# Twelve units of the second feed-forward network: the denominator's linear term and product on VectorE, and another order of the last three token tiles

## The chip, the cores and the metric

The kernel runs on one core of a Trainium2 chip. The metric is the device time of one execution in microseconds (us). The three runs of the kernel before took 796.35, 797.74 and 798.19 us; their median is 797.74. Times in the text are counted from the start of the span, the time from the first to the last instruction of the profiled execution.

## The reference

Attention, a mixture of experts and a second feed-forward network follow one another on 1152 tokens of 512 values, all in float32. The change touches the second network alone:

```
h = x @ w_in                                # 1152 x 512 @ 512 x 2048
P = a[0] + a[1]*h + a[2]*h**2 + a[3]*h**3
Q = 1 + |b[0]|*|h| + |b[1]|*h**2
g = P / (Q + 1e-6)
out = g @ w_out                             # 1152 x 2048 @ 2048 x 512
```

## The kernel before

Each factor of a matrix product is split into a high and a low part in a reduced format, and a product is made of three matmuls (high x high, high x low or low x high, and the third). TensorE accumulates in PSUM.

The 2048 hidden values of the second network are worked in four blocks of 512 (`blk` from `NB1`), the tokens in three groups of 384 (`q`), and a block's hidden values in four slices of 128 (`f`). One slice of one group is called a unit here; a block has twelve, numbered 0 to 11 for the first block. For each unit `first` issues twelve matmuls of 384 columns (line 1172) into a PSUM tile `ps_h`, of which there are three, and starts `rational`, which is a generator of three steps. At each new unit `step_stages` takes the third step of the unit two before it, the second of the one before, and the first of the new one, so each engine's queue holds these in that order. Step one: ScalarE makes `ha` = |h| (L1148), `pp` = a3*h + a2 (L1149) and `qq` = c1*|h| + c0 (L1150), the denominator's linear term; VectorE makes the numerator's next factors (L1151, L1152), which read `ps_h`; GpSimd multiplies `qq` by `ha` (L1153). Step two: ScalarE takes Ln and Exp (L1157, L1158) into `rr`, a tile in PSUM, and VectorE refines the reciprocal and makes the quotient (L1159, L1160, L1161). Step three: ScalarE copies the high part (L1163), GpSimd subtracts to get the low part (L1164).

`second` multiplies a group's four slices by `w_out` for one token tile of 128 tokens: twelve matmuls of 512 columns (L1180), the third, sixth, ninth and twelfth with low parts. In the first block ScalarE copies the result to `acc` (L1191); in later blocks VectorE adds it (L1193). In the last block each token tile is sent to the output from SP's queue. Token tiles 4 and 8 need two transfers each (L1199), the others one (L1201).

The first block overlaps the end of the mixture of experts: `down` for the last pair (VectorE's accumulation is L936), and `x2_T`, nine times, once for a token tile: four transpositions (L1207) into a PSUM tile of the same tag `r` and the same two slots as `rr`, a copy on ScalarE (L1209) and a subtraction on VectorE (L1210). The ninth comes after unit 4. From unit 5 on, each of six units also takes one weight chunk (`load_w`): a conversion to the high part on ScalarE (L298) and two subtractions on GpSimd for the low part (L304). The remaining chunks come in the later blocks, or with the units just before them.

The order of instructions is written out by hand; each engine works its queue in order, and waits are put in for data and for free buffers. At the end the three token tiles of the last group (6, 7, 8) are worked together: three slices of each tile, then the fourth slice of tile 6 and its output, of tile 7, of tile 8.

Of the kernel before, what the change touches and what calls it, by code (L numbers as in the profile page):

```python
# [9 lines left out]
F32 = mybir.dt.float32  # L10
# [3 lines left out]
AF = mybir.ActivationFunctionType  # L14
ALU = mybir.AluOpType
# [4 lines left out]
NT, DM = B * S, H * D  # L20
E, FF, FF2 = 4, 1024, 2048
NB = (E * FF + FF2) // 512
NB1 = E * FF // 512
NPAIR = E * FF // 256
P = 128
# [110 lines left out]
class Kernel:  # L136
# [992 lines left out]
    def second_stage(self):  # L1129
        nc, moe, acc = self.nc, self.wmoe, self.acc  # L1130
        self.o_bufs = 3
        x2 = self.xall.rearrange("p (w q k s) -> p w q k s", w=2, q=3, k=4)
        x2 = {q: (x2[:, 0, q], x2[:, 1, q]) for q in range(3)}
        a0, a1, a2, a3 = (self.ab[:, i:i + 1] for i in range(4))
        c0, c1 = self.babs[:, 0:1], self.babs[:, 1:2]

        stages = []

        def step_stages():
            for g in list(stages):  # L1140
                if next(g, True):
                    stages.remove(g)

        def rational(ps, hi, lo):
            def tmp(nm):
                return moe.tile([P, 384], F32, tag=nm, bufs=3, name=nm)
            ha, pp, qq = tmp("ha"), tmp("pp"), tmp("qq")
            nc.scalar.activation(out=ha, in_=ps, func=AF.Abs)  # L1148
            nc.scalar.activation(out=pp, in_=ps, func=AF.Identity, scale=a3, bias=a2)  # L1149
            nc.scalar.activation(out=qq, in_=ha, func=AF.Identity, scale=c1, bias=c0)  # L1150
            nc.vector.tensor_tensor(out=pp, in0=ps, in1=pp, op=ALU.mult)  # L1151
            nc.vector.scalar_tensor_tensor(out=pp, in0=pp, scalar=a1, in1=ps, op0=ALU.add, op1=ALU.mult)  # L1152
            nc.gpsimd.tensor_tensor(out=qq, in0=qq, in1=ha, op=ALU.mult)  # L1153
            yield False

            rr = self.ps.tile([P, 512], F32, tag="r", bufs=2, name="rr")[:, 0:384]
            nc.scalar.activation(out=rr, in_=qq, func=AF.Ln, bias=self.one_eps)  # L1157
            nc.scalar.activation(out=rr, in_=rr, func=AF.Exp, scale=-1.0)  # L1158
            nc.vector.scalar_tensor_tensor(out=qq, in0=qq, scalar=1.0 + 1e-6, in1=rr, op0=ALU.add, op1=ALU.mult)  # L1159
            nc.vector.scalar_tensor_tensor(out=rr, in0=qq, scalar=2.0, in1=rr, op0=ALU.subtract, op1=ALU.mult, reverse0=True)  # L1160
            nc.vector.scalar_tensor_tensor(out=pp, in0=pp, scalar=a0, in1=rr, op0=ALU.add, op1=ALU.mult)  # L1161
            yield False
            nc.scalar.activation(out=hi, in_=pp, func=AF.Copy)  # L1163
            nc.gpsimd.tensor_tensor(out=lo, in0=pp, in1=hi.bitcast(F32), op=ALU.subtract)  # L1164

        def first(blk, q, f):
            ps = self.ps.tile([P, 384], F32, tag="h", bufs=3, name="ps_h")
            (wh, wl), (hi_x, lo_x) = self.w_tiles["u", blk, f // 2], x2[q]
            fo = P * (f % 2)
            for k in range(4):  # L1170
                for i, (w, v) in enumerate(((wh, hi_x), (wh, lo_x), (wl, hi_x))):
                    nc.tensor.matmul(ps, lhsT=w[:, k, fo:fo + P], rhs=v[:, k, :], start=(k == i == 0), stop=(k == 3 and i == 2))  # L1172
            stages.append(rational(ps, *self.h_tiles(blk, q, f)))
            step_stages()

        def second_part(ps, blk, q, tt, f):
            hh, hl = self.hs[blk, q, f]
            wh, wl = self.w_tiles["d", blk, f // 2]
            for i, (a, w) in enumerate(((hh, wh), (hh, wl), (hl, wh))):
                nc.tensor.matmul(ps, lhsT=a[:, P * tt:P * tt + P], rhs=w[:, f % 2, :], start=(f == i == 0), stop=(f == 3 and i == 2))  # L1180

        def second(blk, q, tt):
            ps = self.ps.tile([P, DM], F32, tag="o", bufs=3, name="ps_o")
            for f in range(4):
                second_part(ps, blk, q, tt, f)
            second_out(ps, blk, q, tt)

        def second_out(ps, blk, q, tt):
            tok = 3 * q + tt
            if blk == NB1:  # L1190
                nc.scalar.activation(out=acc[:, tok], in_=ps, func=AF.Copy)  # L1191
            else:
                nc.vector.tensor_tensor(out=acc[:, tok], in0=ps, in1=acc[:, tok], op=ALU.add)  # L1193
                if blk == NB - 1:
                    out = self.t["out"]
                    if tok in (4, 8):
                        for to, rows in self.token_rows(out):
                            if to[1] == tok:
                                nc.sync.dma_start(out=rows, in_=acc[to])  # L1199
                    else:  # L1200
                        nc.sync.dma_start(out=out[P * tok:P * tok + P, :], in_=acc[:, tok])  # L1201

        def x2_T(q, tt):
            xh, xl = x2[q]
            ps = self.ps.tile([P, 4, P], F32, tag="r", bufs=2, name="ps_x")
            for k in range(4):
                nc.tensor.transpose(ps[:, k, :], acc[:, 3 * q + tt, P * k:P * k + P], self.ident)  # L1207
            sl = slice(P * tt, P * tt + P)
            nc.scalar.activation(out=xh[:, :, sl], in_=ps, func=AF.Copy)  # L1209
            nc.vector.tensor_tensor(out=xl[:, :, sl], in0=ps, in1=xh[:, :, sl].bitcast(F32), op=ALU.subtract)  # L1210

        units = [(blk, q) for blk in range(NB1, NB) for q in range(3)]
        F = [u + (f,) for u in units for f in range(4)]
        total = len(F)
        loads = []

        def up():
            blk, q, f = F.pop(0)
            first(blk, q, f)
            if loads:  # L1220
                loads.pop(0)()
            if (q, f) == (2, 3):
                loads.extend([self.load_w] * 2)

        def lead(n):
            while F and total - len(F) < n:
                up()


        p = NPAIR - 1  # L1230
        self.down(p - 1, 7)
        self.down(p - 1, 8)
        self.load_w()
        self.load_w()
        for t in range(9):
            self.down(p, t)
            if t:
                x2_T((t - 1) // 3, (t - 1) % 3)
            if t in (2, 4):
                self.load_w()  # L1240
            if t > 4:
                up()
        up()
        x2_T(2, 2)
        loads = [self.load_w] * 6
        for i, (blk, q) in enumerate(units[:-1]):
            for tt in range(3):
                lead(4 * i + tt + 7)
                if not F:
                    step_stages()  # L1250
                    step_stages()
                second(blk, q, tt)
            lead(4 * i + 9)
            if q == 2:
                loads.extend([self.load_w] * 2)

        blk, q = units[-1]
        ps = [self.ps.tile([P, DM], F32, tag="o", bufs=3, name="ps_o") for _ in range(3)]
        while stages:
            step_stages()  # L1260
        for tt in range(3):
            for f in range(3):
                second_part(ps[tt], blk, q, tt, f)
        for tt in range(3):
            second_part(ps[tt], blk, q, tt, 3)
            second_out(ps[tt], blk, q, tt)


@with_exitstack
# [46 lines left out]
```

## Time and profile before

| what | value |
|---|---|
| median of three runs | 797.74 us (796.35 to 798.19) |
| span of the profiled execution | 795.7 us |
| TensorE busy in the span | 774.5 us (97%) |
| VectorE, ScalarE, GpSimd busy | 647.8, 477.1, 467.5 us |
| mean granted clock of TensorE | 0.997 |
| last addition on VectorE ends | 791.96 us |

The profiled execution's own time is known as its span, 795.7 us, 2.04 us under the median of the runs. Busy shares are means over stages with different limits; the second network stands from about 583 us to the end. Matmuls overlap, so that a matmul's modelled end lies after the start of the next.

### The profile page before, as it was taken

What the parts mean: (1) busy time and instruction counts of PE and PEld (TensorE: products, weight loads), DVE (VectorE), ACT (ScalarE), POOL (GpSimd) and SP (SyncE); (2) the same over time, 40 slices, a digit from 0 to 9 for tenths busy, and PEclk for the clock granted to TensorE, in tenths of its full rate; (3) what the DMA queues carried; (4) which work ended last, traced back from release to release, by engine and by line L of the source; (5) the groups of instructions that cost most, each with busy time, mean ns of one, the idle gap of its engine ahead of it and who ended that gap; (6) DMA issues with size and microseconds to landing.
All of it is one profiled execution on the core that took longest, in us unless ns stands there. A gap on an engine that the chain in (4) does not pass through costs nothing.

```text
span 795.7 us, 13247 instructions
## 1 busy us (share of the span) xinstructions
PE 774.5 (97%) x4756; PEld 680.7 (86%) x4756; DVE 647.8 (81%) x1207; ACT 477.1 (60%) x940; POOL 467.5 (59%) x456
## 2 busy tenths in 40 slices
PE   6998999999999999999999999999999999999997
PEld 2338899998998999899988999889888889999986
DVE  7996899989779888888888888888577667888775
ACT  3878999999433333343333333333279998887772
POOL 4197798987366445555444564444257977754442
PEclk9999999999999999999999999999999999999999
DMA  6797758571014344443434443433131311000012
GB/s 163 266 309 184 205 125 212 116 217 38 22 33 132 120 132 133 133 133 106 130 110 133 133 133 114 137 99 101 41 107 42 118 53 54 2 1 1 0 41 79
DMA packets 70449, 87.63 MB, mean 110 GB/s; under 512 B 34288, under 2 KB 42736, under 8 KB 70256
## 3 DMA queue, kind: packets, MB, share of 16 engines
q1 hardware_dynamic: 69808, 86.63, 36.2%
q8 instruction: 37, 0.61, 0.3%
q14 instruction: 28, 0.23, 0.1%
q10 hardware_dynamic: 576, 0.16, 0.1%
HBM read 60.15 MB, written 21.61 MB: 103 GB/s over the span
## 4 chain that ended last, share of the span: by engine, by line
PE 76%; POOL 6%; ACT 6%; issue 5%; DVE 4%; DMA 2%; SPq 1%; ACTq 0%; POOLq 0%; DVEq 0%
PE ps_o L930 20%; PE ps_y L1022 10%; PE ps_o L1180 10%; PE ps_h L1172 9%; PE ps_x L1022 8%; PE ps L627 5%; PE ps L731 4%; PE ps L687 4%; POOL we L304 2%; PE ps_ab L436 1%; POOL wml L304 1%; PE ps_x L920 1%; DVE hid L426 1%; DMA bias_d<-bo 1%; PE ps L581 1%
## 5 line engine op out<-in xcount | busy, mean ns | idle before, releaser
L930 PE MATMUL ps_o<-we,hs 128*128 128x512 f32 x810 | 203.4, 392 | 0.0
L930 PEld LDWEIGHTS ps_o<-we,hs 128*128 128x128 f32 x810 | 146.0, 188 | 25.8
L304 POOL TENSOR_TENSOR we<-wstg,we 128x512 fp32r<-128x512 f32 x40 | 57.1, 1447 | 130.5 <-ACT we L298 130.5
L936 DVE SCALAR_TENSOR_TENSOR acc<-ps_o,prob,acc 128x512 f32<-128x512 f32 x135 | 99.8, 744 | 30.6 <-PE ps_o L930 30.4
L1153 POOL TENSOR_TENSOR qq<-qq,ha 128x384 f32<-128x384 f32 x48 | 49.0, 1021 | 70.5 <-ACT qq L1150 68.7
L1180 PE MATMUL ps_o<-wmh,hs 128*128 128x512 f32 x252 | 83.5, 392 | 1.1 <-POOL hs L1164 1.1
L1172 PE MATMUL ps_h<-x,wmh 128*128 128x384 f32 x288 | 73.7, 336 | 0.0
L960 ACT ACTIVATE hs<-ps_x 128x576 fp32r<-128x576 f32 x32 | 20.9, 652 | 80.9 <-DVE ps_x L1034 74.1
L669 POOL TENSOR_SCALAR P<-P,ri 128x576 f32<-128x576 f32 x72 | 53.2, 752 | 16.9 <-DVE ri L660 8.5
L641 DVE CUSTOM_DVE_ANT_0 P<-ps,bias 128x576 f32<-128x576 f32 x72 | 53.6, 750 | 9.1 <-PE ps L627 8.4
L649 ACT ACTIVATE P<-P,nm 128x576 f32<-128x576 f32 x72 | 56.0, 780 | 4.0 <-DVE nm L641 3.7
L1159 DVE SCALAR_TENSOR_TENSOR qq<-qq,rr 128x384 f32<-128x384 f32 x48 | 26.6, 554 | 38.2 <-ACT rr L1158 36.3
L329 POOL TENSOR_TENSOR wu<-wt,wu 128x512 fp32r<-128x512 f32 x28 | 36.3, 1316 | 36.4 <-ACT wu L325 36.4
L1180 PEld LDWEIGHTS ps_o<-wmh,hs 128*128 128x128 f32 x252 | 47.3, 188 | 11.4 <-POOL hs L1164 1.9
L436 PE MATMUL ps_ab<-hid,wm 128*32 128x288 f32 (+18 forms) x352 | 48.1, 496 | 9.1 <-DVE hid L426 7.6
L1172 PEld LDWEIGHTS ps_h<-x,wmh 128*128 128x128 f32 x288 | 52.6, 188 | 2.0
L716 DVE TENSOR_TENSOR ptl<-ps,pth 128x512 fp32r<-128x512 f32 x72 | 48.6, 684 | 5.5 <-ACT pth L712 4.7
L627 PE MATMUL ps<-kh,qs 128*128 128x288 f32 x168 | 50.3, 320 | 1.0 <-DVE nm L641 1.0
L1164 POOL TENSOR_TENSOR hs<-pp,hs 128x384 fp32r<-128x384 f32 x48 | 49.0, 1022 | 3.8 <-issue 2.8
L1180 PE MATMUL ps_o<-wml,hs 128*128 128x512 f32 x126 | 49.5, 393 | 0.0
L1022 PEld LDWEIGHTS ps_y<-x,wu 128*128 128x128 f32 x336 | 47.5, 188 | 2.2
L1022 PEld LDWEIGHTS ps_x<-sums,wu 128*128 128x128 f32 x336 | 47.5, 188 | 2.2
(147 smaller groups left out, 2071.9 us busy)
## 6 DMA issues: line engine op xcount, KB each, us to landing
wstg<-moe_w SPq DMA_DIRECT2D x32, 512.0 KB, 3.9
bias_d<-bo SPq DMA_DIRECT2D x32, 295.5 KB, 4.3
bias<-bias_d SPq DMA_DIRECT2D x16, 576.0 KB, 4.8
w<-moe_w_in SPq DMA_DIRECT2D x16, 512.0 KB, 4.0
w<-moe_w_out SPq DMA_DIRECT2D x16, 512.0 KB, 3.9
kl<-kh SPq DMA_DIRECT2D x16, 288.0 KB, 4.6
w_u<-wmag SPq DMA_DIRECT2D x16, 256.0 KB, 2.4
w_d<-wmag SPq DMA_DIRECT2D x16, 256.0 KB, 2.4
```

Of the source, the lines that this page charges most:

```text
L304: nc.gpsimd.tensor_tensor(out=lo[:, sl], in0=stg[:, sl], in1=hi[:, sl].bitcast(F32), op=ALU.subtract)
L436: nc.tensor.matmul(ps[32 * q:32 * q + 32, i, 0:b - a], lhsT=wm, rhs=hs[q][:, a:b], start=True, stop=True)
L627: nc.tensor.matmul(ps[:, half, dst:dst + w], lhsT=lhs, rhs=k[:, src:src + w], start=(i == 0), stop=(i == len(m) - 1))
L641: nc.vector.tensor_tensor_reduce(out=Pt[u][:, S * h:S * h + S].rearrange("p (a b) -> p a b", a=2), in0=ps[:, :, 0:288], in1=self.bias_t[n ...
L649: nc.scalar.activation(out=pt, in_=pt, func=AF.Exp, scale=-1.0, bias=stat.pop(g), accum_out=sums[n, c][:, h:h + 1])
L669: nc.gpsimd.tensor_scalar(out=pt[:, sl], in0=pt[:, sl], scalar1=ri, scalar2=1.0, op0=ALU.mult, op1=ALU.mult)
L930: nc.tensor.matmul(ps, lhsT=a, rhs=w[:, f, :], start=(f == i == 0), stop=(f == 1 and i == 2))
L936: nc.vector.scalar_tensor_tensor(out=acc[:, t], in0=ps, scalar=pr, in1=acc[:, t], op0=ALU.mult, op1=ALU.add)
L1022: nc.tensor.matmul(ps[:, half, 0:288], lhsT=wu[:, w, i, k], rhs=x[v][:, k, 288 * half:288 * half + 288], start=(start and k == j == 0), st ...
L1153: nc.gpsimd.tensor_tensor(out=qq, in0=qq, in1=ha, op=ALU.mult)
L1172: nc.tensor.matmul(ps, lhsT=w[:, k, fo:fo + P], rhs=v[:, k, :], start=(k == i == 0), stop=(k == 3 and i == 2))
L1180: nc.tensor.matmul(ps, lhsT=a[:, P * tt:P * tt + P], rhs=w[:, f % 2, :], start=(f == i == 0), stop=(f == 3 and i == 2))
```

## The change

In the first block (`blk == NB1`) VectorE makes `qq` in place of ScalarE, with a tensor_scalar, and multiplies it by `ha` in place of GpSimd; both stand ahead of L1151 in VectorE's queue. In the later blocks the work stays where it was, and GpSimd's product is issued before VectorE's two operations in the program text, on its own queue. At the end the three token tiles come in the order 8, 6, 7. Tile 7 is computed in two halves of 256 columns in two PSUM banks (the second is a `ps_h` tile), with twice as many matmuls of half the columns, and each half is added and sent by itself, the first from ScalarE's queue and the second from SP's.

```
-        def rational(ps, hi, lo):
+        def rational(ps, hi, lo, vector):
...
-            nc.scalar.activation(out=qq, in_=ha, func=AF.Identity, scale=c1, bias=c0)
+            if vector:
+                nc.vector.tensor_scalar(out=qq, in0=ha, scalar1=c1, scalar2=c0, op0=ALU.mult, op1=ALU.add)
+                nc.vector.tensor_tensor(out=qq, in0=qq, in1=ha, op=ALU.mult)
+            else:
+                nc.scalar.activation(out=qq, in_=ha, func=AF.Identity, scale=c1, bias=c0)
+                nc.gpsimd.tensor_tensor(out=qq, in0=qq, in1=ha, op=ALU.mult)
             nc.vector.tensor_tensor(out=pp, in0=ps, in1=pp, op=ALU.mult)
             nc.vector.scalar_tensor_tensor(out=pp, in0=pp, scalar=a1, in1=ps, op0=ALU.add, op1=ALU.mult)
-            nc.gpsimd.tensor_tensor(out=qq, in0=qq, in1=ha, op=ALU.mult)
...
-            stages.append(rational(ps, *self.h_tiles(blk, q, f)))
+            stages.append(rational(ps, *self.h_tiles(blk, q, f), blk == NB1))
...
-        def second_part(ps, blk, q, tt, f):
+        def second_part(ps, blk, q, tt, f, cols=slice(0, DM)):
...
+                nc.tensor.matmul(ps, lhsT=a[:, P * tt:P * tt + P], rhs=w[:, f % 2, cols], start=(f == i == 0), stop=(f == 3 and i == 2))
...
-        ps = [self.ps.tile([P, DM], F32, tag="o", bufs=3, name="ps_o") for _ in range(3)]
...
-        for tt in range(3):
-            for f in range(3):
-                second_part(ps[tt], blk, q, tt, f)
-        for tt in range(3):
-            second_part(ps[tt], blk, q, tt, 3)
-            second_out(ps[tt], blk, q, tt)
+        order = (2, 0, 1)
+        ps = {tt: self.ps.tile([P, DM], F32, tag="o", bufs=3, name="ps_o") for tt in order}
+        halves = [ps[1][:, 0:256], self.ps.tile([P, 384], F32, tag="h", bufs=3, name="ps_h")[:, 0:256]]
...
+        for tt in order:
+            for f in range(3):
+                part(tt, f)
+        for tt in order[:2]:
+            part(tt, 3)
+            second_out(ps[tt], blk, q, tt)
+        tok = 3 * q + 1
+        for i, half in enumerate(halves):
+            cols = slice(256 * i, 256 * i + 256)
+            second_part(half, blk, q, 1, 3, cols)
+            nc.vector.tensor_tensor(out=acc[:, tok, cols], in0=half, in1=acc[:, tok, cols], op=ALU.add)
+            (nc.scalar, nc.sync)[i].dma_start(out=self.t["out"][P * tok:P * tok + P, cols], in_=acc[:, tok, cols])
```

`part(tt, f)` calls `second_part` once for tiles 8 and 6, and for tile 7 once for each half.

## Rows read from the trace of the kernel before

**Rows 1.** Busy time by engine in two stretches of the second network.

```profile
582.00:641.00 59.00, 57.62 (x303) 52.15 (x301) 42.70 (x75) 53.63 (x99) 45.71 (x43) 1.00 0.22 72
641.00:780.00 139.00, 138.78 (x699) 125.71 (x698) 109.85 (x193) 112.08 (x213) 80.78 (x80) 1.00 0.07 24
```

**Rows 2.** The chain of waits from 700 us on: start, us, what.

```profile
777.59 12.30 PE ps_o L1180 x54
...
789.91 2.05 DVE acc L1193 x3
```

**Rows 3.** Waits of PE after 560 us: us, times, longest.

```profile
PE ps_o L1180 <- POOL hs L1164: 1.1, 2, 0.9
```

**Rows 4.** Timeline, 589 to 600 us: start, us, engine, line, operation, idle before.

```profile
589.41 0.55 DVE L1159 SCALAR_TENSOR_TENSOR qq<-qq,rr 128x384 f32<-128x384 f32 x1 [0.49 <-ACT rr L1158]
...
594.08 0.56 DVE L1160 SCALAR_TENSOR_TENSOR rr<-qq,rr 128x384 f32<-128x384 f32 x1
...
594.68 0.61 DVE L1161 SCALAR_TENSOR_TENSOR pp<-pp,ab,rr 128x384 f32<-128x384 f32 x1
...
595.21 0.55 DVE L1151 TENSOR_TENSOR pp<-ps_h,pp 128x384 f32<-128x384 f32 x1
...
598.76 0.61 DVE L1161 SCALAR_TENSOR_TENSOR pp<-pp,ab,rr 128x384 f32<-128x384 f32 x1
...
599.43 0.66 PE L1207 MATMUL ps_x<-ident,acc 128*128 128x128 f32 x4 [0.24 <-DVE pp L1161]
```

**Rows 5.** Timeline of the stretch with weight conversions.

```profile
613.18 0.56 DVE L1159 SCALAR_TENSOR_TENSOR qq<-qq,rr 128x384 f32<-128x384 f32 x1 [1.47 <-ACT rr L1158]
...
613.91 0.71 ACT L1150 ACTIVATE qq<-ha,babs 128x384 f32<-128x384 f32 x1
...
614.51 1.06 ACT L298 ACTIVATE wmh<-wstg 128x1024 fp32r<-128x1024 f32 x1
...
614.90 0.55 DVE L1151 TENSOR_TENSOR pp<-ps_h,pp 128x384 f32<-128x384 f32 x1
...
616.34 2.52 POOL L304 TENSOR_TENSOR wml<-wstg,wmh 128x512 fp32r<-128x512 f32 x2
...
616.41 0.58 ACT L1157 ACTIVATE rr<-qq,one_eps 128x384 f32<-128x384 f32 x1
...
617.61 0.56 DVE L1159 SCALAR_TENSOR_TENSOR qq<-qq,rr 128x384 f32<-128x384 f32 x1 [1.51 <-ACT rr L1158]
...
624.36 0.50 PE L1180 MATMUL ps_o<-wmh,hs 128*128 128x512 f32 x1 [0.87 <-POOL hs L1164]
...
635.45 0.56 DVE L1159 SCALAR_TENSOR_TENSOR qq<-qq,rr 128x384 f32<-128x384 f32 x1 [1.55 <-ACT rr L1158]
...
640.46 1.02 POOL L1164 TENSOR_TENSOR hs<-pp,hs 128x384 fp32r<-128x384 f32 x1
```

**Rows 6.** Groups of VectorE by line and shape: count, busy us, mean ns.

```profile
L426 DVE TENSOR_SCALAR hid<-dtab,shift 128x384 f32<-128x384 f32 x7 | 2.5, 411 | 0.0
...
L988 DVE TENSOR_TENSOR u<-u,u 128x576 f32<-128x576 f32 x2 | 1.5, 748 | 0.0
```

**Rows 7.** Timeline, GpSimd and VectorE side by side at 34 and 213 us.

```profile
33.74 18.43 DVE L426 TENSOR_SCALAR hid<-dtab,shift 128x304 f32<-128x304 f32 x54
...
36.77 21.94 POOL L560 TENSOR_SCALAR splk<-rawk 128x576 fp32r<-128x576 f32 x1 [4.02 <-PE ps L581]
...
212.91 3.35 POOL L304 TENSOR_TENSOR wdl<-wstg,wdh 128x512 fp32r<-128x512 f32 x2 [3.69 <-ACT wdh L298]
...
213.38 1.73 DVE L988 TENSOR_TENSOR m<-m,m 128x576 f32<-128x576 f32 x1
```

**Rows 8.** Last issues on SP, then issues by size: KB each, us to landing.

```profile
791.99 1.13 SPq L1199 DMA_DIRECT2D out<-acc  x2
...
out<-acc SPq DMA_DIRECT2D x7, 256.0 KB, 2.1
out<-acc SPq DMA_DIRECT2D x4, 128.0 KB, 2.3
```

More of the change, by code (lines that the diff above doesn't have):

```diff
@@ L1179, in second_part @@
             for i, (a, w) in enumerate(((hh, wh), (hh, wl), (hl, wh))):
-                nc.tensor.matmul(ps, lhsT=a[:, P * tt:P * tt + P], rhs=w[:, f % 2, :], start=(f == i == 0), stop=(f == 3 and i == 2))
+                nc.tensor.matmul(ps, lhsT=a[:, P * tt:P * tt + P], rhs=w[:, f % 2, cols], start=(f == i == 0), stop=(f == 3 and i == 2))
         def second(blk, q, tt):
@@ L1257, in second_stage, with part @@
         blk, q = units[-1]
-        ps = [self.ps.tile([P, DM], F32, tag="o", bufs=3, name="ps_o") for _ in range(3)]
         while stages:
             step_stages()
-        for tt in range(3):
+        order = (2, 0, 1)
+        ps = {tt: self.ps.tile([P, DM], F32, tag="o", bufs=3, name="ps_o") for tt in order}
+        halves = [ps[1][:, 0:256], self.ps.tile([P, 384], F32, tag="h", bufs=3, name="ps_h")[:, 0:256]]
+        def part(tt, f):
+            if tt != 1:
+                second_part(ps[tt], blk, q, tt, f)
+            else:
+                for i, half in enumerate(halves):
+                    second_part(half, blk, q, tt, f, slice(256 * i, 256 * i + 256))
+        for tt in order:
             for f in range(3):
-                second_part(ps[tt], blk, q, tt, f)
-        for tt in range(3):
-            second_part(ps[tt], blk, q, tt, 3)
+                part(tt, f)
+        for tt in order[:2]:
+            part(tt, 3)
             second_out(ps[tt], blk, q, tt)
+        tok = 3 * q + 1
+        for i, half in enumerate(halves):
+            cols = slice(256 * i, 256 * i + 256)
+            second_part(half, blk, q, 1, 3, cols)
+            nc.vector.tensor_tensor(out=acc[:, tok, cols], in0=half, in1=acc[:, tok, cols], op=ALU.add)
+            (nc.scalar, nc.sync)[i].dma_start(out=self.t["out"][P * tok:P * tok + P, cols], in_=acc[:, tok, cols])
 @with_exitstack
```

## The prediction

> **What bounds the kernel now.** I read the table of engines by stretch first. The columns are busy time and count of PE, PEld, DVE, ACT and POOL, then the granted clock, the DMA share and GB/s. In both stretches of the second feed-forward network TensorE is busy nearly all the time at a granted clock of 1.00, the 2.4 GHz level (57.62 of 59 us, 138.78 of 139) [rows 1]. The chain of waits then shows what sets the end: 54 matmuls of line 1180 follow one another for 12.30 us, three VectorE additions end 2.05 us after them, and output transfers come last [rows 2]. So there are two places to gain: idle TensorE in the network's first block, and what follows its last matmul. The waits of TensorE say how much idle time there is: the matmuls of line 1180 waited 1.1 us for GpSimd's low parts, twice [rows 3]. One was before the matmul at 624.36 [rows 5]. Read from start to start, about 1.4 us were lost, since a matmul's successor normally starts before its modelled end. Just before that stands a third, smaller wait, of a transposition at 599.43 for VectorE's line 1161 [rows 4].
>
> The timeline of the first block then tells which queue is late. From 607 to 633 each unit (one 128-row slice of hidden values for 384 tokens; twelve in the block) also brings a weight conversion, six in all. L1159 of one unit stands at 613.18 and of the next at 617.61 [rows 5]: 4.43 us a unit, with ScalarE and GpSimd full (45.71 of 59 us for POOL over the whole stretch, most of it here) [rows 1]. TensorE eats its lead up and waits. The change takes one operation off each of these two queues, which is why it might help.
>
> **The change part by part.**
>
> *First block, prices.* For 12 units it removes a ScalarE activation (0.60 us from its start at 613.91 to the next at 614.51 [rows 5]) and a GpSimd product. It adds to VectorE, ahead of L1151, a tensor_scalar of 128x384 from SBUF to SBUF, 0.41 us in another line's rows [rows 6], and a product of two SBUF tiles. The product is not in the trace at this width. At 576 columns it takes 0.75 us undisturbed [rows 6], and the product with one operand in PSUM takes 0.55 at 384 (L1151 [rows 4]); I take 0.55, with 0.41 and 0.75 as bounds. An operation that needs its predecessor starts 0.04 us after its end (594.08+0.56 to 594.68), one that doesn't starts 0.08 before it (594.68 to 595.21 for 0.61 us) [rows 4]. So VectorE gets 0.45 + 0.46 = 0.91 us more per unit when nothing blocks it.
>
> *First block, before the conversions.* Until 600 us VectorE has nothing to spare. It also carries the first network's accumulations and the low parts of its transposed output, and its only idle time there is 0.49 us before L1159 of unit 0 [rows 4]. What is queued behind the new operations is L1151, the accumulation, and the whole next unit. Units 0 to 2 come before the ninth transposition, which waits for the PSUM slot that L1161 of unit 2 releases. Unit 0's addition meets the idle time, and its product is done sooner than GpSimd's was: carried through the queue, L1159 of unit 0 comes 0.14 us sooner. Units 1 and 2 add 0.91 each. L1161 of unit 2 moves by 1.68, from 598.76 to 600.44, and the transposition from 599.43 to 601.1 [rows 4]: +1.7 us on TensorE, which stands in order behind it.
>
> *First block, with the conversions.* A VectorE operation with two SBUF inputs and a GpSimd operation don't run side by side in this trace. L988 from 213.38 took 1.73 us where its like takes 0.75, because L304 on GpSimd ran; two L304 took 3.35 us from 212.91 where two take 2.52 [rows 5, 7]. Whoever comes first holds, and the waiting one goes next. A tensor_scalar does the same: one GpSimd operation of 128x576 lasted 21.94 us beside 54 of them in an unbroken row [rows 7]. The kernel's other VectorE work in this stage reads one operand from PSUM, and shows no such stretching. The Trainium skill, page "SBUF — State Buffer", section "SBUF: two separate sides", calls this pair of ports an exclusive lock held for a whole instruction, and counts a VectorE operation in a two-port mode or with two SBUF inputs. The trace agrees, by those 1.73 and 21.94 us. If only the product held it, unit 5 would lose 1.4 us less below and each of five later units 0.16, so that the sum would end 2.2 us lower.
>
> Now one unit, from its L1159 (613.18 = 0) [rows 5]. The tensor_scalar takes the place of L1151, at 1.72, and ends at 2.13. The conversion on ScalarE moves up by the removed activation to 0.73, ends at 1.79, and L304 asks at about 1.86: it waits for the tensor_scalar, gets the ports, and holds them for 1.27. The product, wanted at 2.17, starts near 3.2 to 3.4 and ends 3.7 to 3.95. Ln waits for it, and L1159 follows Ln by 1.20 (616.41 to 617.61). So a unit takes 4.95 to 5.2 us where it took 4.43; I take 4.95, because the ends of overlapping operations in rows 7 show that the ports change hands a little before the recorded end. Without a conversion the same sum is 1.72 + 0.45 + 0.55 + 0.04 + 1.20 = 3.95.
>
> Carried forward from L1161 of unit 2 at 600.44: tensor_scalar and product of unit 3 end at 601.95, its L1159 starts at 603.2. Unit 4 takes 3.95 and 0.4 for the ninth token tile's low part, 607.6. In unit 5 L304 asks first and both new operations wait, 5.8: 613.4. Units 6 and 7 take 4.95 each: 623.3. The low part of unit 7 starts 4.8 later, after both L304 and the product between them, and takes 1.02: TensorE gets it at 629.2 and not at 624.36 [rows 5], +4.8. Units 8 to 10 take 4.95 each, unit 11 3.95: L1159 of unit 11 at 642.1, not 635.45. Its low part follows as before by 5.0 (635.45 to 640.46 [rows 5]), since unit 12 has the old form: 647.1, +6.7. From there on TensorE bounds again [rows 1], and the lag stays. Term: +6.7 us, its ends +4.2 (product 0.41, or early hand-over) and +8.5 (product 0.75). The removed activation gains nothing: ScalarE now waits for the product.
>
> *The tail.* Before, the last addition (three of 0.68) ends at 791.96, and token tile 8, last, leaves by two issues on SP from 791.99 (1.13 us together, so the second starts at 792.53) and lands 2.3 later, 794.83; the span ends 0.87 after that [rows 2, 8]. Now tile 8 goes first, tile 7 last, in two halves. TensorE issues 24 matmuls of 256 columns for 12 of 512: nothing more at best (the array's pace of 0.23 us per 512, 12.30/54 [rows 2]), and I take 0.06 in all. VectorE needs about 0.42 for each half (0.68 for 512 columns [rows 2] and 0.55 for 384 [rows 4], carried on to 256) and so ends near 792.0, no sooner. SP issues tile 8's pair from 790.63 to 791.8, tile 6 until 792.2, and the last half then; the first half has ScalarE's idle queue. Landing takes 2.1 to 2.3 [rows 8], so 794.3 to 794.5. I take -0.4, with 0 (narrow rows land later) and -0.8 as ends.
>
> **Sum.** 795.70 + 6.7 - 0.4 = 802.0 us of span. The median of the runs is 2.04 above the profiled span (797.74 against 795.70), so 804.0 us; with the ends, 801 to 806.
>
> **The rivals.** A: the ports cost nothing here, say because the requests fall clear of each other. Then 0.91 per unit is hidden, a unit takes 3.95, low parts are ready before TensorE wants them, and the waits of rows 3 vanish in the lag of 1.7 that the ninth transposition leaves: +0.3 net, 797.6 with the tail. For it: over 59 us GpSimd is idle for 13 [rows 1]. Against: in the conversion stretch L304 and the two new operations come 0.1 to 0.3 us apart, every unit. The Trainium skill, page "GPSIMD Engine Reference", section "Engine selection", prefers VectorE for elementwise work with two inputs. The rows agree on the price alone (512 columns: 1.27 us for one L304, 0.68 for one L1193 [rows 2, 5]), and by that rule alone this rival is the sum.
>
> B, faster: besides A's free ports the ninth transposition isn't delayed, and 1.4 of waiting and 0.4 of tail go: 795.9. For it: the change takes 0.60 us a unit off a full ScalarE, ahead of everything VectorE waits for. It decides at 0.17 us for both new operations together: twice that less 0.14 is what L1161 of unit 2 moves by, and above 0.2 of delay the gain falls under 1.6. Against: one of them alone has a row of 0.41 [rows 6].
>
> C, slower still: in every conversion L304 asks first, as in unit 5, and both new operations wait. Each of five more units costs 0.88: +4.4, 808.4. The margin is narrow: the tensor_scalar starts at 1.72, L304 asks at 1.86.
>
> D: the waits put into the program take the two halves of tile 7 for one region, so that the second addition waits for the first half's transfer, 2.1 us [rows 8]; it adds 2 to any of these and lies in the range.
>
> **How the numbers follow.** Forecast 0.70, A 0.14, B 0.08, C 0.08. About 0.2% (1.6 us) is what a measurement of this kernel can tell from no change. Faster comes from B alone, 0.08; the same from A, 0.14; slower from the forecast and C, 0.78. The range 797.2 to 807.6 holds the forecast with its ends and most of A, and leaves B and C out; the forecast's own range is 801 to 806.
>
> **What would show it.** Right: the ninth transposition waits until about 601 for L1161; in units 5 to 10 the new product lasts 1.3 us or more and the first L304 about 1.4; L1159 comes every 4.9 to 5.2 us; TensorE waits for low parts near 629 and 647, and for a PSUM slot before them; VectorE's last addition ends within 0.1 of where it did after the last matmul, and the last landing 0.3 to 0.5 sooner. Wrong: a product of 0.55 beside L304 (A), or a ninth transposition before 600 (B).

## The result, and the profile after

The changed kernel takes 804.54 us (median of five runs, 803.75 to 805.60); the kernel before, beside it, 798.04 us (796.35 to 798.73). The ratio is 1.0079, 95% interval 1.0067 to 1.0091: 6.3 us slower, 5.3 to 7.3, as forecast. The profiled execution has a span of 802.0 us. In the changed kernel the new tensor_scalar is L1151, the new product L1152; L1161 is Ln, L1163 to L1165 are the three operations of the reciprocal (L1159 to L1161 before), L1168 is the low part, L1176 and L1184 are the two matmul lines, L1211 the transpositions.

Single executions reach the second network at times that differ by up to 2 us: unit 0's first matmul starts at 582.99 before and at 582.06 after. Two stretches don't suffer from that. From unit 0's first matmul to the start of the first of the three last additions of token tiles it took 206.92 us before (582.99 to 789.91) and 213.68 after (582.06 to 795.74): +6.76. From there to the end of the span it took 5.79 and 6.22: +0.43. These are called the block stretch and the tail below.

The waits of TensorE after 560 us (us in total, times, longest) show new names:

```profile
PE ps_o L1184 <- POOL hs L1168: 2.2, 2, 1.2
PE ps_x L1211 <- DVE pp L1165: 1.9, 1, 1.9
PE ps_h L1176 <- DVE pp L1157: 1.5, 2, 1.1
```

Before, there were two waits of 1.1 us in all for low parts [rows 3] and 0.5 us at transpositions; these are 5.6 us of idle engine. The second line is the ninth transposition. The timeline (start, us, engine, line, operation, idle before) has it 0.95 us later than before, in a span that began its second network 0.93 earlier [rows 4], and the unit's matmuls behind it are slow:

```profile
599.71 0.61 DVE L1165 SCALAR_TENSOR_TENSOR pp<-pp,ab,rr 128x384 f32<-128x384 f32 x1
...
600.38 0.66 PE L1211 MATMUL ps_x<-ident,acc 128*128 128x128 f32 x4 [1.95 <-DVE pp L1165]
...
600.79 3.48 PE L1176 MATMUL ps_h<-x,we 128*128 128x384 f32 x12
```

In a conversion unit (the timeline again; rows 5 show the same stretch of before) the tensor_scalar starts, L304 asks and waits for it, and the product waits for L304:

```profile
613.39 1.07 ACT L298 ACTIVATE wmh<-wstg 128x1024 fp32r<-128x1024 f32 x1
613.78 0.62 DVE L1165 SCALAR_TENSOR_TENSOR pp<-pp,ab,rr 128x384 f32<-128x384 f32 x1
614.31 0.48 DVE L1151 TENSOR_SCALAR qq<-ha,babs 128x384 f32<-128x384 f32 x1
614.54 2.97 POOL L304 TENSOR_TENSOR wml<-wstg,wmh 128x512 fp32r<-128x512 f32 x2 [2.24 <-ACT wmh L298]
614.82 1.53 DVE L1152 TENSOR_TENSOR qq<-qq,ha 128x384 f32<-128x384 f32 x1
...
616.38 0.59 ACT L1161 ACTIVATE rr<-qq,one_eps 128x384 f32<-128x384 f32 x1 [1.02 <-DVE qq L1152]
...
617.51 0.55 DVE L1163 SCALAR_TENSOR_TENSOR qq<-qq,rr 128x384 f32<-128x384 f32 x1
```

The product lasts 1.53 us, undisturbed 0.56 (units 0 to 4 and 11). Two L304 last 2.97 where they took 2.52 [rows 5]; with the pair under way their operations lie end to end, not side by side. (Alone, tensor_scalar, L304, product and L304 take 0.48, 1.26, 0.56 and 1.26 us, 3.56 together; from 614.31 to the end of L304 at 617.51 it is 3.20. So each change of hands comes about 0.1 us before the recorded end, an estimate from these figures.) L1163 comes 4.92 us after the one before (612.59), and so in units 6 to 10, where it was 4.43 to 4.47. TensorE meets the result four times. These rows of the timeline begin with a wait, two for a PSUM slot and two for a low part:

```profile
622.44 0.61 PE L1176 MATMUL ps_h<-x,wmh 128*128 128x384 f32 x2 [1.05 <-DVE pp L1157]
628.35 0.51 PE L1184 MATMUL ps_o<-wmh,hs 128*128 128x512 f32 x1 [1.00 <-POOL hs L1168]
641.13 0.61 PE L1176 MATMUL ps_h<-x,wmh 128*128 128x384 f32 x2 [0.42 <-DVE pp L1157]
647.24 0.51 PE L1184 MATMUL ps_o<-wmh,hs 128*128 128x512 f32 x1 [1.20 <-POOL hs L1168]
```

The last of them is for unit 11's low part, which GpSimd makes here (rows 5 have it at 640.46 before):

```profile
646.20 0.99 POOL L1168 TENSOR_TENSOR hs<-pp,hs 128x384 fp32r<-128x384 f32 x1
```

At the end, the last additions and the last issues on SP:

```profile
795.74 1.39 DVE L1197 TENSOR_TENSOR acc<-ps_o,acc 128x512 f32<-128x512 f32 x2 [4.84 <-PE ps_o L1184]
797.04 0.41 DVE L1285 TENSOR_TENSOR acc<-ps_o,acc 128x256 f32<-128x256 f32 x1
797.38 0.41 DVE L1285 TENSOR_TENSOR acc<-ps_h,acc 128x256 f32<-128x256 f32 x1
```

```profile
796.46 1.12 SPq L1203 DMA_DIRECT2D out<-acc  x2
797.68 0.54 SPq L1205 DMA_DIRECT2D out<-acc  x1
798.31 0.52 SPq L1286 DMA_DIRECT2D out<-acc  x1
```

The additions end 2.05 us after the first begins, exactly as before [rows 2]. The last half is issued at 798.31 and lands at 801.13, 2.82 us later; tile 6, issued at 797.68, lands 3.1 us later.

### The profile page after: what moved, and what is told of

Read it like the earlier page. It is cut to its first block, busy times and chain, and to the rows that moved or that the text cites. A ratio compares the mean times of both kernels' runs of the same rounds, so it can differ in the third digit from the quotient of the medians.

```text
span 802.0 us, 13261 instructions
## 1 busy us (share of the span) xinstructions
PE 776.1 (97%) x4768; PEld 682.2 (85%) x4768; DVE 665.9 (83%) x1232; ACT 470.2 (59%) x928; POOL 457.1 (57%) x444
## 4 chain that ended last, share of the span: by engine, by line
PE 77%; DVE 9%; ACT 6%; issue 4%; POOL 3%; DMA 2%; SPq 0%; DVEq 0%; ACTq 0%; POOLq 0%
PE ps_o L930 20%; PE ps_y L1022 10%; PE ps_o L1184 10%; PE ps_h L1176 9%; PE ps_x L1022 8%; PE ps L627 4%; PE ps L731 4%; PE ps_ab L436 4%; PE ps L687 3%; DVE qq L1152 2%; DVE hid L426 1%; POOL we L304 1%; ACT P L649 1%; PE ps L581 1%; PE ps_x L920 1%
## 5 line engine op out<-in xcount | busy, mean ns | idle before, releaser
L304 POOL TENSOR_TENSOR we<-wstg,we 128x512 fp32r<-128x512 f32 x40 | 57.4, 1456 | 131.4 <-ACT we L298 130.4
L1184 PE MATMUL ps_o<-wmh,hs 128*128 128x512 f32 (+1 forms) x252 | 83.1, 389 | 2.2 <-POOL hs L1168 2.2
L1176 PE MATMUL ps_h<-x,wmh 128*128 128x384 f32 x288 | 74.4, 339 | 1.5 <-DVE pp L1157 1.5
L1155 POOL TENSOR_TENSOR qq<-qq,ha 128x384 f32<-128x384 f32 x36 | 36.7, 1018 | 59.6 <-ACT qq L1154 57.8
L1168 POOL TENSOR_TENSOR hs<-pp,hs 128x384 fp32r<-128x384 f32 x48 | 49.9, 1040 | 21.2 <-ACT hs L1167 18.2
L1184 PEld LDWEIGHTS ps_o<-wmh,hs 128*128 128x128 f32 x252 | 47.4, 188 | 12.2 <-POOL hs L1168 3.0
L1176 PEld LDWEIGHTS ps_h<-x,wmh 128*128 128x128 f32 x288 | 52.9, 190 | 4.1 <-DVE pp L1157 2.1
L1022 PEld LDWEIGHTS ps_y<-sums,wu 128*128 128x128 f32 x336 | 47.5, 188 | 2.2
L1184 PE MATMUL ps_o<-wml,hs 128*128 128x512 f32 (+1 forms) x126 | 49.1, 390 | 0.0
```

The source lines that it names most:

```text
L304: nc.gpsimd.tensor_tensor(out=lo[:, sl], in0=stg[:, sl], in1=hi[:, sl].bitcast(F32), op=ALU.subtract)
L1022: nc.tensor.matmul(ps[:, half, 0:288], lhsT=wu[:, w, i, k], rhs=x[v][:, k, 288 * half:288 * half + 288], start=(start and k == j == 0), st ...
```

## The experiments

Theory P is that of the prediction: ports that VectorE and GpSimd take in turn, and a delayed ninth transposition. Its rivals are put in each expectation. All kernels are changes of the first block with the old end, but for the two whose names begin with tail and for late_best. Block stretch and tail are measured as above, in each kernel's profiled execution. The last column tells when GpSimd ends unit 11's low part, counted from the start of unit 0's first matmul. The ratios compare each kernel with runs of the kernel before in the same round; the medians come from different rounds.

| kernel | median us | ratio to before, 95% | block stretch us | tail us | unit 11's low part us |
|---|---|---|---|---|---|
| before | 797.5 to 798.0 | | 206.92 | 5.79 | 58.49 |
| changed | 804.54 | 1.0079 (1.0067 to 1.0091) | 213.68 | 6.22 | 65.12 |
| first_only | 804.65 | 1.0069 (1.0044 to 1.0093) | 213.54 | 5.96 | 65.11 |
| tail_only | 798.34 | 0.9997 (0.9980 to 1.0014) | 207.02 | 5.89 | 58.48 |
| psum_product | 800.13 | 1.0016 (0.9999 to 1.0033) | 208.92 | 5.97 | 60.19 |
| late_both | 800.69 | 1.0025 (1.0009 to 1.0040) | 209.87 | 5.78 | 61.44 |
| early_both | 799.89 | 1.0021 (0.9996 to 1.0046) | 209.48 | 5.79 | 61.06 |
| linear_only | 802.77 | 1.0062 (1.0039 to 1.0084) | 211.70 | 5.96 | 63.22 |
| product_only | 797.20 | 0.9992 (0.9971 to 1.0013) | 206.81 | 5.79 | 57.84 |
| late_best | 796.68 | 0.9983 (0.9967 to 1.0000) | 205.69 | 6.03 | 56.71 |
| late3_product | 795.97 | 0.9982 (0.9973 to 0.9990) | 205.26 | 5.79 | 56.27 |
| tail_alone | 797.03 | 0.9997 (0.9986 to 1.0007) | 207.00 | 4.92 | 58.45 |

The prediction took unit 11's low part to set how late TensorE is. The last column bears that out. In the changed kernel, first_only, late_both, early_both and linear_only it shifts by 6.63, 6.62, 2.95, 2.57 and 4.73 us, and the block stretch grows by 6.76, 6.62, 2.95, 2.56 and 4.78. In the changed kernel 0.10 us of the 6.76 stands in tail_only too, so it belongs to the new end. In product_only, late_best and late3_product the low part comes early, and TensorE doesn't wait for it.

**first_only.** The old end in the changed kernel:

```
-        order = (2, 0, 1)
...
+        for tt in range(3):
+            second_part(ps[tt], blk, q, tt, 3)
+            second_out(ps[tt], blk, q, tt)
```

> The first-block edit alone; the last three token tiles as before. Theory P (ports: the two new operations and GpSimd's L304 take turns, and VectorE's added work before unit 3 delays the ninth transposition): the whole loss of the changed kernel stands here, +6 to +7 us on the kernel before (804 to 805), with the ninth transposition waiting about 2 us, the product lasting about 1.5 us in units 5 to 10, and waits of TensorE for low parts near 628 and 647. The stretch from the first of the last three additions to the end of the span is then as before, 5.8 us. Rival T (a good part of the loss is at the end of the kernel): +4 us or less here. The granted clock should fall to 0.5 for about 3.4 us after the ninth transposition's wait, as in the changed kernel, if that wait causes it.

The block stretch grew by 6.62 us, the product took 1.50 to 1.54 us in units 5 to 10. The tail is 5.96, 0.17 over the kernel before with the same code, so that this much is scatter (it stands behind the last landing; see the tail kernels below). The loss stands in the first block; rival T falls. The granted clock stayed at 1.00 after the transposition's wait, unlike in the changed kernel; more on that below.

**psum_product.** In first_only, the second new operation and one of its inputs:

```
-                nc.vector.tensor_tensor(out=qq, in0=qq, in1=ha, op=ALU.mult)
+                nc.vector.tensor_tensor(out=qq, in0=ps, in1=qq, op=ALU.max)
```

> As first_only, but the second new VectorE operation reads its other input from PSUM: a maximum of ps_h and qq stands in the place of the product of qq and ha (the product with |h| is left out). VectorE has the same number of operations of the same size; only that one no longer reads two SBUF inputs. Theory P: the operation takes 0.55 us beside L304 in place of 1.53, L1163 (the first of the reciprocal's three) comes every 4.0 to 4.3 us in units 6 to 10, the wait for unit 11's low part is gone or below 0.3 us, and the time is +1.9 to +2.5 us on the kernel before (about 800.2), most of it the ninth transposition's delay of 2 us. Rival W (VectorE's added work sets the pace, whatever it reads): +6 to +7 us, as first_only.

The timeline of one conversion unit:

```profile
617.47 0.48 DVE L1151 TENSOR_SCALAR qq<-ha,babs 128x384 f32<-128x384 f32 x1
617.71 2.65 POOL L304 TENSOR_TENSOR wml<-wstg,wmh 128x512 fp32r<-128x512 f32 x2 [0.39 <-ACT wmh L298]
618.05 0.56 DVE L1152 TENSOR_TENSOR qq<-ps_h,qq 128x384 f32<-128x384 f32 x1
```

and its only waits of TensorE after 560 us:

```profile
PE ps_x L1211 <- DVE pp L1165: 2.0, 1, 2.0
PE ps_x L1211 <- DVE acc L936: 0.2, 1, 0.2
```

The operation ran beside L304, 0.56 us and not 1.53. Units 6 to 10 took 4.02 us. The block stretch is +2.00. VectorE had as many operations of the same size as in first_only, so 4.6 of the 6.6 us come from what the operation reads, and rival W falls. Of the 2.00 us that remain, unit 11's low part shifts by 1.70, and TensorE comes to it 0.3 later still, without a wait. TensorE had been 2.07 us late at the ninth transposition and 3.65 behind the next unit's matmuls, which ran at a lower clock (last section). How much of the 0.3 is the clock's no run separates.

**late_both and early_both.** In first_only,

```
-            stages.append(rational(ps, *self.h_tiles(blk, q, f), blk == NB1))
+            stages.append(rational(ps, *self.h_tiles(blk, q, f), blk == NB1 and 4 * q + f >= 5))
```

and `< 5` in the other.

> As first_only, but units 0 to 4 keep the old form; VectorE takes both operations in units 5 to 11 alone. Theory P: the ninth transposition waits as in the kernel before (0.3 us, at 599.4) and the granted clock stays at 1.00 there, but units 5 to 10 keep their pace of 4.9 to 5.0 us, so +3.5 to +4 us on the kernel before (about 802). If the delay of the ninth transposition were the whole loss: 0 to -1.5 us, since the conversions are then harmless. Rival W: 7 of 12 units, about +4 as well, but with products of 0.56 us.

> As first_only, but only units 0 to 4 have the new form; units 5 to 11 keep the old one; old tail. It separates the delay of the ninth transposition from the conversions. Theory P: that transposition waits 2 us more than before, as in first_only, the units after it keep the old pace of 4.4 to 4.5 us, and since the chain of units is late by then as well, the waits for low parts remain in part: +2 to +2.8 us (800 to 800.7). Rival: the lag of 2 us swallows the waits for low parts: +0.5 us. The granted clock may fall to 0.5 after that wait.

late_both: +2.95 us, less than expected. The transposition started as before and units 5 to 10 took 4.92, but unit 5 did not lose the extra 0.8 us that it loses in the changed kernel, since in late_both its tensor_scalar (605.58) came before L304 (605.74). early_both: +2.56; its units 6 to 10 have the old pace of 4.43 to 4.47 and the waits for low parts shrink to 0.2 us, within what theory P expected, and its rival (+0.5) falls. So either part alone costs 2.6 to 3.0 and both 6.6: they add up, and 1.1 us more, of which unit 5 is 0.8. Neither delay hides the other: both stand in the one chain of units that ends in unit 11's low part, whose shift is the loss in either (2.95 and 2.57).

**linear_only and product_only.** The two halves of the edit:

```
                 nc.vector.tensor_scalar(out=qq, in0=ha, scalar1=c1, scalar2=c0, op0=ALU.mult, op1=ALU.add)
-                nc.vector.tensor_tensor(out=qq, in0=qq, in1=ha, op=ALU.mult)
+                nc.gpsimd.tensor_tensor(out=qq, in0=qq, in1=ha, op=ALU.mult)
```

```
-                nc.vector.tensor_scalar(out=qq, in0=ha, scalar1=c1, scalar2=c0, op0=ALU.mult, op1=ALU.add)
+                nc.scalar.activation(out=qq, in_=ha, func=AF.Identity, scale=c1, bias=c0)
                 nc.vector.tensor_tensor(out=qq, in0=qq, in1=ha, op=ALU.mult)
```

> One half of the first-block edit: VectorE makes the linear term (tensor_scalar), GpSimd keeps the product; old tail. Theory P, carried through the queues: the product on GpSimd now follows a term that VectorE makes late, so L304 of the next chunk stands ahead of it; units 5 to 10 take about 4.9 us, the wait for unit 7's low part is above 3 us, and the loss is +4.5 to +5.5 us (about 803) though VectorE gets only 0.48 us a unit more and no operation with two SBUF inputs. Rival W (added VectorE work sets the loss): half of the whole edit's, +3 us or less.

> The other half: ScalarE keeps the linear term, VectorE makes the product of two SBUF tiles in all twelve units; old tail. Theory P: ScalarE's term is ready before L304 of the same unit asks, so the product mostly gets the ports first; units 5 to 10 stay at 4.3 to 4.5 us, the ninth transposition waits 1.5 to 1.8 us for L1165's like, and that lag swallows the two waits for low parts: within 0.5 us of the kernel before (797.5 to 798.5). Rival W2 (any product with two SBUF inputs beside L304 costs 1 us a unit): units at 4.9 us and +4 us or more.

By itself the smaller half does the harm. linear_only: +4.78 us, with units of 4.73 to 4.80 and one wait of 3.3 us for unit 7's low part. Its timeline:

```profile
613.38 1.02 POOL L1168 TENSOR_TENSOR hs<-pp,hs 128x384 fp32r<-128x384 f32 x1
613.88 0.73 DVE L1151 TENSOR_SCALAR qq<-ha,babs 128x384 f32<-128x384 f32 x1
...
614.69 1.02 POOL L1152 TENSOR_TENSOR qq<-qq,ha 128x384 f32<-128x384 f32 x1 [0.30 <-DVE qq L1151]
...
615.67 2.55 POOL L304 TENSOR_TENSOR wml<-wstg,wmh 128x512 fp32r<-128x512 f32 x2
615.75 0.59 ACT L1161 ACTIVATE rr<-qq,one_eps 128x384 f32<-128x384 f32 x1 [0.88 <-POOL qq L1152]
```

The term that ScalarE made early now waits in VectorE's queue behind three operations of the unit before, then 0.26 us for GpSimd; GpSimd, which was full, stands idle 0.30 for it, and Ln 0.88. product_only: -0.11 us. The term is ready early, so the product starts before L304 asks:

```profile
614.45 0.55 DVE L1152 TENSOR_TENSOR qq<-qq,ha 128x384 f32<-128x384 f32 x1
614.92 0.55 DVE L1156 TENSOR_TENSOR pp<-ps_h,pp 128x384 f32<-128x384 f32 x1
615.28 2.56 POOL L304 TENSOR_TENSOR wml<-wstg,wmh 128x512 fp32r<-128x512 f32 x2 [0.86 <-ACT wmh L298]
```

Four of its six conversion units show 0.55, two 0.9. Its gain (no wait for low parts is left) pays for 1.4 us of waiting at the ninth transposition. So a product with two SBUF inputs is no loss by itself; when it asks is what counts. The two halves do not add up to the whole edit's 6.6, since the product stands on GpSimd in one and asks early in the other. Rivals W and W2 fall.

**tail_only and tail_alone.** The change's end in the kernel before; and the same without sending tiles 6 and 8:

```
-                if blk == NB - 1:
+                if blk == NB - 1 and q < 2:
```

> The new order and the split of the last tile alone; the first block as before. The prediction's term was -0.4 us. The trace of the changed kernel says otherwise: from the first of the last three additions to the end of the span it has about 6.2 us where the kernel before has 5.8, since the last transfers land 2.8 to 3.1 us after their issue and not 2.1 to 2.3. Theory L (late landing of the last transfers, which are under way together): +0.3 to +0.6 us in that stretch, and a time that cannot be told from the kernel before. Rival: -0.4 there, if the late landing came from something else in that run.

> As tail_only, but token tiles 6 and 8 are not sent (their part of the output is left out), so that the two halves of tile 7 travel alone. Theory L (the last transfers land late because the last tiles are under way together): the last half is issued at the end of its addition and lands 2.0 to 2.2 us later, not 2.5 to 2.8, and the stretch from the first of the last additions to the end of the span falls to 5.0 to 5.2 us. Rival (a transfer of 256 columns is slower by itself, for its rows are half as long): 2.5 us or more as before, and 5.4 us or more.

tail_only: 5.89 us, 0.10 over the kernel before, where theory L had +0.3 to +0.6 and its rival -0.4; the last half landed 2.49 us after its issue. Over runs it cannot be told from the kernel before. What lies behind the last landing scatters from 0.8 to 1.1 us, so that the stretch from the first of the last additions to the last landing tells more: 4.88 to 4.89 us in the eight kernels with the old end, 5.06 in tail_only, 5.14 in late_best, 5.39 in the changed kernel. tail_alone has the last half issued at 791.03 in 0.34 us,

```profile
791.03 0.34 SPq L1282 DMA_DIRECT2D out<-acc  x1
```

```profile
DMA to landing us min/median/max: 1.8/1.8/1.8
```

and a tail of 4.92. Both figures lie under theory L's 2.0 to 2.2 and 5.0 to 5.2, and its rival falls: a half is not slow by itself, but with the transfers of the other two tiles under way. That alone does not explain it, since the kernel before has three tiles under way as well and lands them in 2.1 to 2.3 us. Its issues begin 0.54 to 0.68 us apart, those of tail_only 0.19 to 0.63. That the spacing makes the difference is argued, not shown, and why the same end lands 0.33 us later in the changed kernel than in tail_only is open. The last landing comes 4.17 us after the first of the three tiles' issues in the kernel before, 4.33 in tail_only, 4.67 in the changed kernel: the new orders did not bring the last landing forward.

**late_best and late3_product.** The product on VectorE from unit 5 on (late_best, with the order 8, 6, 7 unsplit and tile 6 sent from ScalarE's queue), and from unit 3 on with the old end, which is product_only with one line changed:

```
-            stages.append(rational(ps, *self.h_tiles(blk, q, f), blk == NB1))
+            stages.append(rational(ps, *self.h_tiles(blk, q, f), blk == NB1 and 4 * q + f >= 3))
```

> A version meant to beat both kernels. VectorE makes the product of two SBUF tiles in units 5 to 11 alone, ScalarE keeps the linear term; at the end the order is 8, 6, 7 with tile 7 whole, tile 6 sent from ScalarE's queue. Theory P: the ninth transposition waits 0.3 us as before, units 5 to 10 take 4.3 to 4.45 us, the wait for unit 7's low part falls from 1.0 us to 0.3 or less and that for unit 11's goes: -1.1 to -1.4 us in the stretch from the first block to the last additions. Tail: the last issue on SP is at the end of the last addition and alone, and lands 2.1 to 2.5 later, -0.3 to -0.6 us. In all 796.0 to 796.6. Rival W2: the products wait for L304 as in late_both, and it is 1 to 3 us slower than the kernel before.

> The product alone on VectorE, in units 3 to 11, with two SBUF inputs; ScalarE keeps the linear term in all; old tail. Theory P: nothing before the ninth transposition changes, so it starts at 599.4 as before, and the wait for unit 7's low part, 0.3 us more than normal spacing in late_best, is gone as well, since units 3 and 4 have gained 0.3 us: -1.3 to -1.5 us from the first block to the last additions. With the old tail at 5.8 to 6.0 us that is 796.1 to 796.6. Rival: the early product collides with VectorE's late work for the ninth token tile and that transposition or the next units come later: within 0.5 us of the kernel before.

late_best gained 1.23 us in the block stretch, as expected, and lost 0.24 in the tail, where 0.3 to 0.6 less had been expected: its last transfer, which stood behind no other issue on SP, landed 3.06 us after its own. That refutes my reading that SP's queue of issues sets the tail, and agrees with tail_alone. late3_product: -1.66 us in the block stretch, a little more than the 1.3 to 1.5 expected, 795.97 us, ratio 0.9982 (0.9973 to 0.9990). No wait for a low part is left:

```profile
PE ps_x L1211 <- DVE pp L1165: 0.2, 1, 0.2
PE ps_x L1211 <- DVE acc L936: 0.2, 1, 0.2
```

It beats the kernel before by 1.5 us (0.8 to 2.2 by the interval). It was not run beside the changed kernel, which lost 6.3 to the kernel before.

## Why the prediction was right, and where it was not

- *Time and sign.* 804.0 was forecast and 804.54 measured, 802.0 of span and 802.0 measured. The span agrees in part by chance: the term for the block was +6.7 (measured +6.76), that for the tail -0.4 (measured +0.43), and this execution's second network began 0.93 us early; the last two cancel to 0.1. Against the kernel before the runs give +6.5 by their medians where +6.3 was forecast.
- *Ports.* Right, and shown: psum_product takes the conflict away and 4.6 us with it. The pace forecast was 4.95 us a unit, 5.8 in unit 5; 4.92 and 5.71 were measured. Rival C did not come: its narrow margin (0.14 us) held, and the tensor_scalar started 0.23 to 0.29 us ahead of L304 in units 6 to 10. Rival A's pace of 3.95 is nearly what psum_product shows (4.02), so that in the pace it failed on the ports alone; its net of +0.3 us would have failed without them too (psum_product: +2.00 in the block stretch). One reading went too far: "the waiting one goes next" held in these units, but not in the row that the prediction cites beside it (last section).
- *Ninth transposition.* Right in kind, sized too small: L1165 of unit 2 to the transposition as forecast, but the tensor_scalar took 0.475 us and not the 0.41 of another line, so units 1 and 2 brought 0.98 each and it came 1.9 us later, not 1.7 (600.38 + 0.93 against 599.43). The edit in units 0 to 4 alone costs 2.56 (early_both).
- *TensorE's stations.* With the 0.93 us added, TensorE got unit 7's low part at 629.28 (forecast 629.2), and unit 11's began at 647.13 (forecast 647.1), with waits for a PSUM slot ahead of both. That these agree within 0.1 is partly luck: the chain started 0.2 us later than forecast, and then ran 0.09 us faster in unit 5 and 0.03 in each of the five after it. The prediction also has no term for TensorE's lower clock behind the ninth transposition; in the changed kernel it cost nothing in the end, as the last section shows.
- *"The removed activation gains nothing".* Right for the whole edit. The prediction did not see that the shorter operation is by itself the harmful one: it priced the two operations by their lengths, and the linear term's price is that it comes later, not that it is long.
- *The tail.* Wrong. The failing step is "Landing takes 2.1 to 2.3": it took 2.8, and 3.1 for tile 6. The last half was also issued 0.28 us later than forecast (2.57 us after the first of the last additions, not 2.29), as tile 6's issue took 0.54 us on SP and not 0.4. Together these turn the term of -0.4 into the measured +0.43. VectorE's end was forecast within 0.1 and came so. Rival D is refuted: the second addition started 0.33 us after the first.

## What to carry to other kernels

Before work is moved to a less busy engine, look at where its operands lie and at who needs the same ports at that moment; here an operation of one size cost 0.56 or 1.53 us, by one input. Ask when the moved operation can start in its new queue rather than how long it takes: a term of 0.48 us that had been early became late and cost 4.8 us, while the longer product, whose inputs were early, could be moved at a gain once the units that lead up to a tight wait (the ninth transposition's) were left alone. At the end of a kernel time the landing of what is under way together; an earlier issue need not mean an earlier end.

## What the runs showed of the hardware beyond that

TensorE's granted clock fell from its 2.4 GHz level to the 1.2 GHz one after the ninth transposition's wait (columns as in rows 1):

```profile
596.00:600.00 4.00, 2.43 (x14) 2.11 (x13) 3.90 (x8) 2.02 (x4) 1.11 (x1) 1.00 0.00 0
600.00:602.00 2.00, 1.62 (x10) 1.63 (x11) 1.93 (x5) 1.15 (x3) 1.04 (x1) 0.92 0.00 0
602.00:606.00 4.00, 4.00 (x17) 4.00 (x16) 3.82 (x8) 3.09 (x7) 1.28 (x2) 0.61 0.00 0
```

The engine had started nothing for 2.29 us and then took 3.48 us for twelve matmuls that take 2.36 at the upper level (unit 5 of the kernel before, at 599.84). In early_both and psum_product it fell as well, after waits of 2.29 and 2.35 us, and the twelve matmuls took 3.87 and 3.82:

```profile
601.70 3.87 PE L1176 MATMUL ps_h<-x,we 128*128 128x384 f32 x12
600.78 3.82 PE L1176 MATMUL ps_h<-x,we 128*128 128x384 f32 x12
```

In first_only a wait of 2.29 us was not followed by a fall. There the clock fell later, after one of 2.85 us. The two kernels' block stretches differ by 0.14 us all the same: what the slower matmuls lose is given back at the next waits, for which TensorE would have been early. Counted from unit 0's first matmul, TensorE is 3.44 us behind the kernel before once the slow matmuls are done in the changed kernel and 1.88 at the same place in first_only; behind unit 11's low part both are 6.63.

The prediction's "the waiting one goes next" has an exception in the kernel before. A GpSimd operation that takes 0.69 us at the median asked at 36.77 and lasted 21.94, through the rest of the 54 tensor_scalars of rows 7 and the 14 that followed, up to 58.18 (in the second row: smallest, median and largest duration in ns):

```profile
52.08 6.10 DVE L426 TENSOR_SCALAR hid<-ltab,shift 128x576 f32<-128x576 f32 x14
L560 POOL TENSOR_SCALAR splk<-rawk x8: 677/689/21944, 7.2 to 154.1; 128x576 fp32r<-128x576 f32 x8
```

In the conversion units L304 got in between the tensor_scalar and the product each time. There the second VectorE operation needs the first one's result; that this is what lets GpSimd in is not shown.

VectorE's tensor_scalar with one operand column per scalar took 0.475 us at 128x384 here and 0.41 on line 426; what makes the difference was not tried. Nor was a kernel in which L304 asks first in every unit (rival C); unit 5, where it does, shows 1.27 and 1.53 us for the two operations.
